# Converting 20 of 36 weight blocks to halved numbers by a shift and a sign function

## Chip, cores and metric

One core of one Trainium2 chip runs the whole program. The metric is the device time of one execution in microseconds (us), the median of several runs. Engines are named as in the profile: PE is TensorE (PEld its weight loads), DVE is VectorE, ACT is ScalarE, POOL is GpSimd, SP is the engine that issues most DMAs.

## What is computed

Attention over 4 batches, 8 heads, 576 positions and a head size of 64, in which each row keeps only its 32 largest scores; then a dense gated layer `(x @ w_a) * (x @ w_b) @ w_out`; then a routed layer, in which each token goes to the one of 8 experts whose embedding is nearest.

```python
scores = q @ k.T / sqrt(D)                       # per batch and head
kth = partition(scores, -32)[..., -32]
attn = softmax(where(scores >= kth, scores, -1e9))
x = (attn @ v) as 2304 x 512
x = ((x @ w_a) * (x @ w_b)) @ w_out              # d_ff = 1536
e = argmax(normed(x) @ normed(expert_emb).T / tau)
out = gate * (relu(x @ w1[e]) @ w2[e])
```

`w_a`, `w_b`, `w_out` arrive as 64-bit floating-point numbers; all else is of 32 bits.

## The kernel before

The work runs in three stages. In the first, 144 rows of attention (a row is 128 queries against 576 keys) pass through all engines in a pipeline. For each row TensorE makes the scores (L373), ScalarE copies them out of PSUM (`s<-tr`, L374), VectorE finds the 32 largest by four MAX8 and three MATCH_REPLACE8 (L394, L397) and sets a threshold `bi` (L399), ScalarE and POOL apply it and the softmax (L406, L409, L411), TensorE turns the weights (L428) and ScalarE copies them (`wt<-tr`, L431). Each fourth or fifth row closes with the product with `v` (L469), which ScalarE copies too (L472, L457). The dense layer (`moe1`, 9 groups of 256 tokens, 12 column blocks `f` in each) is woven into the rows' gaps on TensorE, and the routing of its tokens follows. The last stage is the experts, after the attention is over.

The order of instructions on PE, DVE, ACT and POOL in the first stage is written out by the program itself (`manual_schedule`): the main loop goes through 144 steps and in each step calls pieces of each row's work in fixed slots. SP's queue is ordered by priorities. An engine works through its queue strictly in order.

The weights of the dense layer are converted once, beside the first 36 or so rows, in 36 blocks of 128x512 numbers (`Blocks`): `order` is a0, b0, a1, b1, then six blocks of `w_out` (o0 to o5), then a2, b2, o6, a3, b3, o7 and so on, at last a11, b11. Below, a, b and o stand for `w_a`, `w_b` and `w_out`. Each block takes these steps:

- SP loads the block (`fetch`, L523) into one of two buffers `raw64`. The load of a block waits until all readers of the block two before it are done.
- ScalarE takes the upper three bits of each number's low word (`w64r<-raw`, L543, the low half of a 32-bit word).
- VectorE shifts the high word left by 3 and clears the two upper bits (`w64t<-raw`, L546), and takes sign and upper exponent bit from the high word into the upper half of `w64r` (L547).
- POOL adds both as whole numbers (`x1T<-w64t,w64r`, L551): that is the number in 32 bits.
- ScalarE rounds it (`wab` or `wo<-x1T`, L559), TensorE forms the rest (L562, L563), ScalarE copies that (L564), and SP stores blocks of a and b to DRAM (`wab_d`, L566).

The steps of a block are called from the main loop: `conv.open()` runs the first one (L543) in slot 3 of a step, just ahead of a copy of scores; `conv.start()` runs VectorE's at the step's end; `conv.stage()` runs the rest in slots 0, 2 and 4. Until step 16 a block is taken up every second step, then two a step.

The gated product is made at L743 (L741 for the first two blocks of the first group): a copy of both products `a` and `b` out of PSUM into `gab`. The layer's output is copied out of PSUM in `route` (L773).

Of the kernel before, what the change touches and what calls it, by code (L numbers as in the profile page):

```python
# [10 lines left out]
F32 = mybir.dt.float32  # L11
F32R = mybir.dt.float32r
BF16 = mybir.dt.bfloat16
I32 = mybir.dt.int32
I16 = mybir.dt.int16
U32 = mybir.dt.uint32
AF = mybir.ActivationFunctionType
OP = mybir.AluOpType
# [50 lines left out]
OB = 3  # L69
NTF = 1  # L70
RGL = 0.8
ET = 0
FX = (0, 5)
EK = 1
# [13 lines left out]
def fused_kernel(  # L88
# [18 lines left out]
    pe, dve, act, pool, sp = nc.tensor, nc.vector, nc.scalar, nc.gpsimd, nc.sync  # L107
# [4 lines left out]
    NT, DM = out.shape  # L112
# [94 lines left out]
    with ExitStack() as ph:  # L207
# [292 lines left out]
        class Blocks:  # L500
# [34 lines left out]
            def block(self, k):  # L535
                i, f = self.order[k]
                raw = self.raw[k]
                if raw.dtype == F32:
                    x = raw
                else:  # L540
                    lo, hi = raw[:, :, :, 0], raw[:, :, :, 1]
                    r = wk.tile([P, KC, P, 2], I16, name="w64r", bufs=TB)
                    act.activation(r[:, :, :, 0], lo.bitcast(U32), AF.Copy, scale=2.0**-29)  # L543
                    yield
                    t = wk.tile([P, KC, P], I32, name="w64t", bufs=TB)
                    dve.tensor_scalar(t, hi, 3, 0x3FFFFFFF, op0=OP.logical_shift_left, op1=OP.bitwise_and)  # L546
                    dve.tensor_scalar(r[:, :, :, 1], raw.bitcast(I16)[:, :, :, 3], -0x4000, None, op0=OP.bitwise_and)  # L547
                    self.fetch(k + 1 + RB)
                    yield
                    x = mk.tile([P, KC, P], F32, name="x1T", bufs=XB)  # L550
                    pool.tensor_tensor(x.bitcast(I32), t, r.rearrange("p a n t -> p a (n t)").bitcast(I32), op=OP.add)  # L551
                    yield
                if i < 2:
                    wt = mk.tile([P, 2, KC, P], F32R, name="wab", bufs=WB)
                    self.tiles[i, f] = wt
                    hi, lo = wt[:, 0], wt[:, 1]
                else:
                    hi, lo = (wo[:, a, f].rearrange("p (c j) -> p c j", c=KC) for a in range(2))
                act.activation(hi, x, AF.Copy)  # L559
                yield  # L560
                p = ps.tile([P, 512], F32, name="tr", bufs=NTR)
                pe.matmul(p, ident, x.rearrange("p c j -> p (c j)"), start=True, stop=False)  # L562
                pe.matmul(p, minusr, hi.rearrange("p c j -> p (c j)"), start=False, stop=True)  # L563
                act.activation(lo, p.rearrange("p (c j) -> p c j", c=KC), AF.Copy)  # L564
                if i < 2:
                    sp.dma_start(wab_d[i, f], wt.bitcast(F32).rearrange("p a c j -> p (a c j)"))  # L566

            def need(self, *block):
                while not self.ready(*block):
                    self.start()  # L570
                    self.stage()

            def ready(self, *block):
                return block in self.order[: sum(a == 4 for a in self.at)]
# [25 lines left out]
                        self.at[k] += 1  # L600

        conv = Blocks()

        routes = []
        routed = []
# [42 lines left out]
        def moe1(G):  # L648
# [12 lines left out]
            def tick():  # L661
                if pend:
                    pend.pop(0)[1]()  # L663

            def second(f, tiles=(0, 1)):
                while pend and pend[0][0] <= f:
                    tick()
                hi, lo = gs[f]
                if gi == 0:
                    conv.need(2, f)  # L670
                for t in tiles:
                    ts = slice(t * P, (t + 1) * P)
                    if f == 0:
                        px[t] = mp.tile([P, DM], F32, name="x1", bufs=2)
                    for i, (g, w) in enumerate(((lo, 0), (hi, 1), (hi, 0))):
                        pe.matmul(  # L676
                            px[t], g[:, ts], wo[:, w, f], start=(f == 0 and i == 0), stop=(f == NF - 1 and i == 2)
                        )
                    if f == NF - 1:
                        r = route(g0 // P + t, px[t])  # L680
                        next(r)
                        routes.append(r)
                        debt[1] = 0.0
                    tick()
                    yield 0.64
# [22 lines left out]
            for f in range(NF):  # L708
                nxt = todo[1][1] if len(todo) > 1 and todo[1][0] <= now[0] else None
                if f >= (NF - 4 if gi else NF - 1) and nxt:  # L710
                    nxt.inputs()
                if f + LA < NF:
                    G.load()
                elif nxt:
                    nxt.load()
                if gi == 0:
                    conv.begun = f
                    while now[0] < NRW and not (conv.ready(0, f) and conv.ready(1, f)):
                        yield None
                    for i in range(2):  # L720
                        conv.need(i, f)
                    ws[f] = [conv.tiles[i, f] for i in range(2)]
                ab = mk.tile([P, 2, GN], F32, name="gab")
                p = None if f in begun else mp.tile([P, 2, 256], F32, name="ab", bufs=2)
                ps_ = begun[f] if f in begun else [p[:, 0], p[:, 1]]
                for i, wt in enumerate(ws[f]):
                    terms = [(a, x, c) for (a, x) in TERMS1 for c in range(KC) if f not in begun or c == KC - 1]
                    for j, (a, x, c) in enumerate(terms):
                        pe.matmul(  # L729
                            ps_[i],  # L730
                            wt[:, a, c, :],
                            xg[x][:, c, :],
                            start=(j == 0 and f not in begun),
                            stop=(j == len(terms) - 1),
                        )
                        if j % 4 == 3 and (i == 0 or j < 11):
                            tick()
                            yield 4 * N / 2400
                if f in begun:
                    for i in range(2):  # L740
                        act.activation(ab[:, i], ps_[i], AF.Copy)  # L741
                else:
                    act.activation(ab, p, AF.Copy)  # L743
                recent[0] = ab
                yield 4 * N / 2400
                hi = mk.tile([P, GN], F32R, name="gh", bufs=LAG + 2)
                lo = mk.tile([P, GN], F32R, name="gl", bufs=LAG + 2)
                gs[f] = hi, lo
                pend.append((f, lambda: None))
                pend.append((f, partial(pool.tensor_tensor, ab[:, 0], ab[:, 0], ab[:, 1], op=OP.mult)))  # L750
                pend.append((f, lambda: None))
                pend.append((f, partial(act.activation, hi, ab[:, 0], AF.Copy)))
                pend.append((f, lambda: None))
                pend.append((f, partial(pool.tensor_tensor, lo, ab[:, 0], hi.bitcast(F32), op=OP.subtract)))
                if f >= LAG:
                    yield from second(f - LAG)
# [4 lines left out]
            for tiles in ((0,), (1,)) if gi == len(GROUPS) - 1 else ((0, 1),):  # L761
                for f in range(NF - LAG, NF):
                    for _ in range(6 if nxt else 0):
                        yield next(nxt[2])
                    for _ in range(NTF if tiles[0] >= ET else 0):
                        tail[0]()
                    yield from second(f, tiles)

        def route(ch, p):
            tk = mk.tile([P, 2], I32, name="tk", bufs=4)  # L770
            token_ids(tk, ch)
            xr = mk.tile([P, RW], F32, name="xr")
            act.activation(xr[:, :DM], p, AF.Copy)  # L773
            x1T = mk.tile([P, KC, P], F32, name="x1T", bufs=XB)
            st = mk.tile([P, 8], F32, name="st")
            act.activation(x1T.rearrange("p c j -> p (c j)"), xr[:, :DM], AF.Square, accum_out=st[:, 0:1])
# [75 lines left out]
        def background(budget, final=False):  # L852

            debt[0] = min(debt[0] + budget, DEBT) if not final else final
            while debt[0] > 0 and (todo or (final and routes)):
# [15 lines left out]
                spent[0] += used  # L871
                if routes and debt[1] > (RGL if todo and todo[0][1].gi == len(GROUPS) - 1 else RGAP):
                    debt[1] = 0.0
# [66 lines left out]
        for step in range(-AHEAD_L, NRW + TL + 5):  # L940
# [64 lines left out]
            i = step - (TL0 if step < S1 else TL)  # L1005
            if i != turned[0] + 1:
                i = -1
# [37 lines left out]
            if 0 <= i < NRW:  # L1045
                next(tg, None)
                b, pr, part, first, last, kind, c, slot = rows[i]
                t = live.pop(i)
# [26 lines left out]
    with ExitStack() as ph:  # L1075
# [52 lines left out]
        def bank(name):  # L1128
            turns[name] += 1
            return banks[turns[name] % len(banks)].tile([P, 512], F32, name=name, bufs=2 if name == "h" else 1)  # L1130
# [189 lines left out]
        for e in range(1, NE):  # L1320
            r = NE - e
# [13 lines left out]
            if e + 1 < NE:  # L1335
                yT = wx.tile([P, KC, cap], F32, name="yT", bufs=1)[:, :, :n]
                for d in range(KC):
                    p = bank("y")[:, :n]
# [17 lines left out]
            else:  # L1356
                for t in range(NT3):
                    p = bank("y")
# [90 lines left out]
```

## Time and profile before

| | |
|---|---|
| median of 3 runs | 1251.49 us (1246.62 to 1252.79) |
| profiled execution | 1249.34 us, span of its instructions 1247.5 us |
| PE, PEld | busy 1134.9 (91%), 982.7 (79%) |
| DVE | busy 914.2 (73%), 2015 instructions |
| ACT | busy 822.5 (66%), 1970 instructions |
| POOL | busy 731.1 (59%) |
| mean granted clock of TensorE | 0.966 of 2.4 GHz |

Shares of the whole span mix the three stages: DVE has almost nothing to do after 820 us. The windows view cuts the span into stretches and gives each engine's busy time in each. In the timeline a line has start, duration, engine, source line, operation and operands; `x2` is two instructions back to back, and a bracket at the end is the idle time ahead of the line and what ended it.

### The profile page before, as it was taken

Reading aid. Unit: us, or ns where it says so; the run is one execution under the profiler, and the core shown is the slowest. Engines: PE = TensorE matmul, PEld = TensorE weight load, DVE = VectorE, ACT = ScalarE, POOL = GpSimd, SP = SyncE. Lnnn points to the kernel's source line nnn. Section 1 sums busy time; section 2 is a strip of 40 time slices with the busy share of each in tenths; the row PEclk is TensorE's granted clock in tenths of the full one; section 3 lists DMA queues with packets and bytes.
Section 4 is the critical chain, followed back from the end, with each engine's and each line's share of the span. In section 5 each row is a group of like instructions: output and inputs, shape, how many; then the busy total and the mean of one; then the engine's idle time right before and its main releaser. Section 6 shows DMA issues by size and latency. Waiting matters only on the chain. (4 is left out here: it accounts for less than half of the span.)

```text
span 1247.5 us, 23919 instructions
## 1 busy us (share of the span) xinstructions
PE 1134.9 (91%) x8124; PEld 982.7 (79%) x8125; DVE 914.2 (73%) x2015; ACT 822.5 (66%) x1970; POOL 731.1 (59%) x1195
## 2 busy tenths in 40 slices
PE   5677798999999998999998999899999989999996
PEld 4445566787888887888787888777898868999995
DVE  8998999999999998998999898860110225655540
ACT  5777888888778887777877787663542434555441
POOL 5555698777777876776877677564554420232221
PEclk8788899999999999999999999899999989999998
DMA  7334567667775666667575667557987335565530
GB/s 235 118 123 144 193 198 257 224 215 223 252 228 148 191 222 218 181 203 220 159 204 169 205 191 220 186 155 226 325 296 210 110 124 207 177 218 207 184 102 27
DMA packets 129200, 240.05 MB, mean 192 GB/s; under 512 B 24896, under 2 KB 74176, under 8 KB 129074
## 3 DMA queue, kind: packets, MB, share of 16 engines
q1 hardware_dynamic: 125170, 228.74, 57.9%
q0 software_dynamic: 3904, 9.75, 2.1%
q8 instruction: 65, 1.06, 0.4%
q14 instruction: 61, 0.50, 0.1%
HBM read 198.38 MB, written 40.31 MB: 191 GB/s over the span
## 5 line engine op out<-in xcount | busy, mean ns | idle before, releaser
L394 DVE MAX8 t<-y 128x8 f32<-128x576 f32 x432 | 311.8, 749 | 2.7
L409 POOL TENSOR_TENSOR z<-s,z 128x576 f32<-128x576 f32 x144 | 206.2, 1432 | 73.0 <-ACT z L406 70.3
L397 DVE MATCH_REPLACE8 y<-t,y 128x576 f32<-128x576 f32 x288 | 213.9, 743 | 0.0
L729 PE MATMUL ab<-xg,wab 128*128 128x256 f32 x1398 | 208.8, 288 | 2.5 <-DMA wab<-wab_d 1.2
L729 PEld LDWEIGHTS ab<-xg,wab 128*128 128x128 f32 x1398 | 182.2, 189 | 5.4 <-DMA wab<-wab_d 1.4
L428 PE MATMUL tr<-ident,z 128*128 128x128 f32 x720 | 135.3, 288 | 49.0 <-ACT z L411 44.8
L729 PE MATMUL ab<-raw,wab 128*128 128x256 f32 x1152 | 173.8, 290 | 3.1 <-DMA wab<-wab_d 2.1
L374 ACT ACTIVATE s<-tr 128x288 f32<-128x288 f32 x288 | 117.8, 410 | 58.4 <-PE tr L373 35.1
L729 PEld LDWEIGHTS ab<-raw,wab 128*128 128x128 f32 x1152 | 151.7, 191 | 5.9 <-DMA wab<-wab_d 2.1
L431 ACT ACTIVATE wt<-tr 128x384 f32<-128x384 f32 (+2 forms) x320 | 127.9, 411 | 39.2 <-PE tr L428 38.1
L428 PEld LDWEIGHTS tr<-ident,z 128*128 128x128 f32 x720 | 89.6, 146 | 68.0 <-ACT z L411 56.8
L676 PE MATMUL x<-wo,gh 128*128 128x512 f32 x432 | 136.2, 397 | 0.0
L1155 POOL DMA_INDIRECT out_dram<-o,ids x24 | 33.1, 1378 | 169.7 <-ACT o L1154 118.0
L373 PE MATMUL tr<-kT,qT 128*128 128x288 f32 x512 | 123.8, 327 | 8.2 <-ACT s L374 5.1
L1102 DVE TENSOR_TENSOR u<-raw,u 128x1024 fp32r<-128x1024 f32 x64 | 76.1, 1221 | 69.2 <-ACT u L1101 47.2
L663 POOL TENSOR_TENSOR gl<-gab,gh 128x256 fp32r<-128x256 f32 x108 | 82.8, 767 | 55.0 <-ACT gh L663 45.8
L394 DVE MAX8 t<-s 128x8 f32<-128x576 f32 x144 | 107.0, 743 | 7.6 <-ACT s L374 7.6
L411 ACT ACTIVATE z<-z,bi 128x576 f32<-128x576 f32 x144 | 112.1, 778 | 0.3 <-POOL z L409 0.3
L406 ACT ACTIVATE z<-s,bi 128x576 f32<-128x576 f32 x144 | 111.3, 773 | 0.3 <-DVE bi L399 0.3
L663 POOL TENSOR_TENSOR gab<-gab 128x256 f32<-128x256 f32 x108 | 80.5, 745 | 51.0 <-ACT gab L743 42.8
L397 DVE MATCH_REPLACE8 y<-t,s 128x576 f32<-128x576 f32 x144 | 106.9, 742 | 0.0
L373 PEld LDWEIGHTS tr<-kT,qT 128*128 128x128 f32 x512 | 87.5, 202 | 18.2 <-ACT s L374 5.7
(201 smaller groups left out, 2244.3 us busy)
## 6 DMA issues: line engine op xcount, KB each, us to landing
wab<-wab_d SPq DMA_DIRECT2D x192, 512.0 KB, 4.6
raw<-in_moe_w_dram SPq DMA_DIRECT2D x28, 1024.0 KB, 5.4
wab_d<-wab SPq DMA_DIRECT2D x24, 512.0 KB, 4.7
kT<-kT_d SPq DMA_DIRECT2D x20, 576.0 KB, 5.7
vs<-in_v_dram SPq DMA_DIRECT2D x36, 256.0 KB, 3.1
kT_d<-kT SPq DMA_DIRECT2D x16, 576.0 KB, 4.6
raw<-in_moe_w_a_dram SPq DMA_DIRECT2D x12, 512.0 KB, 4.5
raw<-in_moe_w_b_dram SPq DMA_DIRECT2D x12, 512.0 KB, 4.7
```

What stands on the lines that cost most here:

```text
L373: pe.matmul(p, l, r, start=(i == 0), stop=(i == len(terms) - 1))
L374: act.activation(t.s[:, cs], p, AF.Copy, scale=SCALE)
L394: dve.max(v, cur)
L397: dve.match_replace(out=rest, in_to_replace=v, in_values=cur, imm_value=LOWEST)
L406: act.activation(t.w, t.s, AF.Relu, bias=t.bi[:, 1:2], scale=-HUGE)
L409: pool.tensor_tensor(t.w, t.s, t.w, op=OP.subtract)
L411: act.activation(t.w, t.w, AF.Exp, bias=t.bi[:, 0:1], accum_out=t.o.sm[:, t.slot : t.slot + 1])
L428: pe.transpose(pt[:, i * P : (i + 1) * P], t.w[:, k0 : k0 + P], ident)
L431: act.activation(th[:, sl, w], pv[:, :, src], AF.Copy)
L663: pend.pop(0)[1]()
L676: pe.matmul(px[t], g[:, ts], wo[:, w, f], start=(f == 0 and i == 0), stop=(f == NF - 1 and i == 2))
L729: pe.matmul(ps_[i], wt[:, a, c, :], xg[x][:, c, :], start=(j == 0 and f not in begun), stop=(j == len(terms) - 1),)
```

## The change

Twenty blocks are converted in another way: the twelve of `w_a`, and the first four (`f < F3`, F3 = 4) of `w_b` and of `w_out`. VectorE only shifts, without clearing the two upper bits, and no longer takes sign and exponent bit. In their place ScalarE applies the function Sign to the upper 16 bits of the number, read as bfloat16, and writes +1.0 or -1.0 in bfloat16 to the upper half of `w64r`. POOL's addition is the same; the sum is now half the number. The other 16 blocks stay as they were. Copies that exist already carry a factor 2 in their scale: the copy of `gab` where both products are halved or one is (`f < 4`), and the copy of the layer's output.

```diff
+F3 = 4
...
                     act.activation(r[:, :, :, 0], lo.bitcast(U32), AF.Copy, scale=2.0**-29)
+                    if i == 0 or f < F3:
+                        act.activation(r.bitcast(BF16)[:, :, :, 1], raw.bitcast(BF16)[:, :, :, 3], AF.Sign)
                     yield
                     t = wk.tile([P, KC, P], I32, name="w64t", bufs=TB)
-                    dve.tensor_scalar(t, hi, 3, 0x3FFFFFFF, op0=OP.logical_shift_left, op1=OP.bitwise_and)
-                    dve.tensor_scalar(r[:, :, :, 1], raw.bitcast(I16)[:, :, :, 3], -0x4000, None, op0=OP.bitwise_and)
+                    if i == 0 or f < F3:
+                        dve.tensor_scalar(t, hi, 3, None, op0=OP.logical_shift_left)
+                    else:
+                        dve.tensor_scalar(t, hi, 3, 0x3FFFFFFF, op0=OP.logical_shift_left, op1=OP.bitwise_and)
+                        dve.tensor_scalar(
+                            r[:, :, :, 1], raw.bitcast(I16)[:, :, :, 3], -0x4000, None, op0=OP.bitwise_and
+                        )
                     self.fetch(k + 1 + RB)
...
+        HALVED = 1.0 if w_a.dtype == F32 else 2.0
...
-                        act.activation(ab[:, i], ps_[i], AF.Copy)
+                        act.activation(ab[:, i], ps_[i], AF.Copy, scale=HALVED if f < F3 else 1.0)
...
-                    act.activation(ab, p, AF.Copy)
+                    act.activation(ab, p, AF.Copy, scale=HALVED if f < F3 else 1.0)
...
-            act.activation(xr[:, :DM], p, AF.Copy)
+            act.activation(xr[:, :DM], p, AF.Copy, scale=HALVED)
```

On VectorE, where blocks b2 (buffer 1168) and o6 (1182) are converted at the end of a step. Before:

```order
L397 MATCH_REPLACE y_1187<-t8_1188,y_1187 128x576
L546 TENSOR_SCALAR w64t_1257<-raw64_1168 128x512
L547 TENSOR_SCALAR w64r_1239<-raw64_1168 128x512
L546 TENSOR_SCALAR w64t_1260<-raw64_1182 128x512
L547 TENSOR_SCALAR w64r_1243<-raw64_1182 128x512
L394 MAX t8_1188<-y_1187 128x8
```

And now (lines have moved by 1 to 9; L550 is the shift alone, L552 and L553 the old pair):

```order
L398 MATCH_REPLACE y_1187<-t8_1188,y_1187 128x576
L550 TENSOR_SCALAR w64t_1258<-raw64_1168 128x512
L552 TENSOR_SCALAR w64t_1260<-raw64_1182 128x512
L553 TENSOR_SCALAR w64r_1244<-raw64_1182 128x512
L395 MAX t8_1188<-y_1187 128x8
```

b2 is among the 20, o6 is not: one instruction is gone, and the neighbours stand as before. This is so at all 20 places.

On ScalarE, slot 3 of the step in which the same two blocks are opened. Before:

```order
L431 ACTIVATE wt_1196<-tr_1227 128x2x128
L559 ACTIVATE wo_127<-x1T_1216 128x512
L543 ACTIVATE w64r_1239<-raw64_1168 128x512
L543 ACTIVATE w64r_1243<-raw64_1182 128x512
L374 ACTIVATE s_1220<-tr_1245 128x288
```

And now (L546 is the Sign):

```order
L432 ACTIVATE wt_1196<-tr_1227 128x2x128
L567 ACTIVATE wo_127<-x1T_1216 128x512
L544 ACTIVATE w64r_1239<-raw64_1168 128x512
L546 ACTIVATE w64r_1239<-raw64_1168 128x512
L544 ACTIVATE w64r_1244<-raw64_1182 128x512
L375 ACTIVATE s_1220<-tr_1246 128x288
```

The Sign of b2 stands between the reads of b2 and o6, ahead of the copy of scores. ScalarE has 20 instructions more and nothing else moved; PE and POOL have the same instructions in the same order. SP has as many DMAs, and some neighbours change places.

## Rows read from the trace of the kernel before

**Rows 1.** Windows view: stretch, its length, then busy time of each engine.

```profile
28.00:118.00 90.00, 59.99 (x339) 42.86 (x339) 85.58 (x197) 68.40 (x158) 51.50 (x68) 0.81 0.40 130
118.00:240.00 122.00, 106.50 (x668) 80.15 (x665) 117.21 (x241) 105.39 (x237) 95.66 (x111) 0.97 0.63 212
240.00:820.00 580.00, 552.18 (x4241) 476.69 (x4240) 543.73 (x1262) 450.94 (x1176) 418.27 (x741) 0.98 0.66 202
820.00:1247.00 427.00, 401.57 (x2822) 372.09 (x2820) 144.35 (x254) 182.65 (x370) 150.36 (x250) 0.99 0.56 185
```

**Rows 2.** Waits of ScalarE from 28 to 113: total, times, longest.

```profile
ACT wt L431 <- PE tr L428: 10.7, 15, 1.0
ACT xsb L472 <- PE tr L469: 3.3, 3, 2.2
...
ACT z L411 <- POOL z L409: 0.3, 1, 0.3
```

**Rows 3.** Tile view of w64t and w64r: durations in ns, least, median, most.

```profile
L546 DVE TENSOR_SCALAR w64t<-raw x36: 397/578/1645, 9.0 to 226.2; 128x512 int32<-128x512 int32 x36
L547 DVE TENSOR_SCALAR w64r<-raw x36: 444/464/1678, 9.4 to 227.0; 128x512 int16<-128x512 int16 x36
```

**Rows 4.** Groups of ScalarE's instructions, 0 to 240: busy, mean ns, idle before.

```profile
L374 ACT ACTIVATE s<-tr 128x288 f32<-128x288 f32 x76 | 31.0, 409 | 4.5 <-PE tr L373 4.0
L543 ACT ACTIVATE w64r<-raw 128x512 int16<-128x512 uint32 x36 | 27.5, 788 | 9.8 <-DMA raw<-in_moe_w_a_dram 3.7 <-DMA raw<-in_moe_w_out_dram 3.6 <-DMA raw<-in_moe_w_b_dram 1.6
...
L559 ACT ACTIVATE wab<-x1T 128x512 fp32r<-128x512 f32 x23 | 14.0, 639 | 2.8 <-POOL x1T L551 2.8
...
L457 ACT ACTIVATE xR<-tr 128x256 f32<-128x256 f32 x7 | 2.7, 384 | 1.2 <-PE tr L449 1.2
...
L179 ACT ACT_TABLE_LOAD x1 | 1.3, 1283 | 0.6 <-PEq L1429 0.6
```

**Rows 5.** Timeline of ScalarE, four waits before 75.

```profile
21.66 0.63 ACT L559 ACTIVATE wab<-x1T 128x512 fp32r<-128x512 f32 x1 [2.21 <-POOL x1T L551]
...
26.23 0.60 ACT L564 ACTIVATE wab<-tr 128x512 fp32r<-128x512 f32 x1 [1.29 <-PE tr L563]
...
50.43 0.38 ACT L472 ACTIVATE xsb<-tr 128x256 f32<-128x256 f32 x1 [2.21 <-PE tr L469]
...
72.23 0.38 ACT L472 ACTIVATE xsb<-tr 128x256 f32<-128x256 f32 x1 [0.56 <-PE tr L469]
```

**Rows 6.** Timelines of ScalarE, SP and VectorE at the hand-over near 112.

```profile
112.01 1.41 ACT L543 ACTIVATE w64r<-raw 128x512 int16<-128x512 uint32 x2
...
112.82 0.38 SPq L523 DMA_DIRECT2D raw<-in_moe_w_a_dram  x1
...
118.45 0.62 DVE L546 TENSOR_SCALAR w64t<-raw 128x512 int32<-128x512 int32 x1 [3.02 <-DMA raw<-in_moe_w_a_dram]
```

**Rows 7.** Timelines of VectorE, SP, ScalarE and TensorE at the hand-over near 140.

```profile
137.97 1.00 DVE L547 TENSOR_SCALAR w64r<-raw 128x512 int16<-128x512 int16 x1
138.87 0.40 DVE L546 TENSOR_SCALAR w64t<-raw 128x512 int32<-128x512 int32 x1
...
140.84 0.38 SPq L523 DMA_DIRECT2D raw<-in_moe_w_a_dram  x1
...
146.25 0.78 ACT L543 ACTIVATE w64r<-raw 128x512 int16<-128x512 uint32 x1 [2.01 <-DMA raw<-in_moe_w_a_dram]
...
147.33 0.85 PE L373 MATMUL tr<-kT,qT 128*128 128x288 f32 x2 [3.42 <-ACT s L374]
```

**Rows 8.** Waits of ScalarE for loads, 185 to 240.

```profile
ACT w64r L543 <- DMA raw<-in_moe_w_out_dram: 3.0, 1, 3.0
...
ACT w64r L543 <- DMA raw<-in_moe_w_b_dram: 1.6, 1, 1.6
ACT w64r L543 <- DMA raw<-in_moe_w_a_dram: 0.3, 1, 0.3
```

**Rows 9.** Timeline of TensorE near 227.

```profile
227.72 0.40 PE L373 MATMUL tr<-kT,qT 128*128 128x288 f32 x1 [2.02 <-ACT qT L350]
```

## The prediction

> **What bounds the kernel now.** I read the windows view first, then the waits of ScalarE, then the timeline at the places where one engine releases another. Times below without a unit are microseconds into the span.
>
> The stretches show three regimes [rows 1]. From 820 on VectorE is a third busy and TensorE is at 94%. From 240 to 820 both are full (TensorE 552.18 of 580, VectorE 543.73), so what arrives late at 240 stays late to the end. The conversion of the weights, which is what the change touches, lies before 240. From 28 to 118 VectorE is 95% busy (85.58 of 90) and ScalarE only 76% (68.40), which would make VectorE the bound.
>
> The waits of ScalarE say otherwise [rows 2]. Between 28 and 113 nearly all its idle time is for TensorE: 15 times it has just finished an exponential and waits until TensorE has turned it (10.7 in all), and some other products. Only 0.3 is for POOL, and nothing for VectorE or a DMA. Such a round trip begins and ends on ScalarE, so it does not shrink when VectorE gets faster: in this stretch ScalarE with its round trips runs as a chain of its own, just as fast as VectorE. One hand-over decides which of the two counts. At 112.01 ScalarE reads two blocks back to back. At 112.82, when the first read is over, SP issues the DMA of the next block. VectorE stands still for 3.02 until that block lands and starts at 118.45 [rows 6]. So at 118 VectorE is late because ScalarE was.
>
> After 118 the roles turn. VectorE's mask of a block that keeps it ends when SP issues the next load at 140.84, ScalarE waits 2.01 for that load, and TensorE then waits 3.42 for the scores that ScalarE copies behind it [rows 7]. Here a faster VectorE helps.
>
> **The change part by part.**
>
> *The mask that goes.* 20 of 36 VectorE instructions `w64r<-raw` disappear. Their median is 464 ns, and one that meets POOL at the memory takes 1.00 [rows 3, 7]. The one at 137.97 runs to 138.97, its successor starts at 138.87: 0.10 overlaps. So one is worth 0.36 alone and 0.90 in company. In the timeline 4 of the 20 take 1.00, as at 137.97: 16 x 0.36 + 4 x 0.90 = 9.4 of VectorE time, ten of the 20 before 110.
>
> *The shift that loses its second operation.* `w64t` keeps its operands, and its 397 ns at the least [rows 3] is the time of its 512 elements a partition; no row shows the same shift with one operation. Gain at most 0.1 each (2 in all), loss none that a row suggests; I take 0.
>
> *The sign that comes.* 20 ScalarE instructions are added, each behind its block's `L543` and ahead of a score copy. No row shows this function. It reads and writes 512 elements at the same spacing as `L543`, which takes 788 ns; in a pair the second adds 1.41 - 0.79 = 0.62 [rows 4, 6]. A plain copy of 512 takes 639 ns, 0.15 less [rows 4]. Bounds 0.47 and 0.79 (no overlap); I take 0.62, the row with the same layout. 20 x 0.62 = 12.4 of ScalarE time.
>
> *The scale in the copies.* Score copies `L374` already carry a scale: 409 ns for 288 columns, against 384 for 256 in `L457` without one [rows 4]. That is 25 ns for 32 more columns, so a scale costs nothing.
>
> *Queues.* TensorE and POOL keep every instruction in its place. SP issues as many transfers, with neighbours swapped while blocks are loaded; the loads of the later blocks keep their order. VectorE no longer writes half of `w64r`; POOL's addition then waits for the sign. POOL is a step behind ScalarE, which hides it, except for a block read directly ahead of its addition. I take 0, and up to 1 for the range.
>
> *The sum along the chain.* Three signs lie before 28. ScalarE's waits of 2.21 and 1.29 follow them [rows 5] and take them up. Seven come between 28 and the issue at 112.82. The one near 47 lies ahead of a wait of 2.21 for a product that does not depend on it, the one near 71 ahead of one of 0.56 [rows 5]: these two cost 0 and 0.06. The other five stand ahead of the exponential that starts a round trip, or (the last) ahead of SP's issue itself. 5 x 0.62 = 3.1, so the block that VectorE waits for lands 3.1 later. What VectorE has saved by then only lengthens its wait.
>
> From 118 to 140.84 VectorE is free of waits and loses three masks: 0.36 + 0.36 + 0.90 = 1.6. The load at 140.84 is issued 3.1 - 1.6 = 1.5 later. Behind it ScalarE runs the sign of that very block before it copies the scores: TensorE goes on at 147.33 + 1.5 + 0.6, so 2.1 later. Until about 190 one more mask of 0.90 counts on the way to a load, and the two signs there fall into ScalarE's wait of 3.0 [rows 8]: 1.2 late. The last four signs cost 2.5, of which ScalarE's waits of 0.3 and 1.6 for loads [rows 8] take up 1.9: 1.8 late. TensorE meets this where it waits for ScalarE at 227.72 [rows 9], and carries it to the end. 1249.34 of the profiled execution + 1.8 = **1251.1**. That execution lies 2.15 below the median of the three runs (1251.49), which spread over 6.2, so about 0.5% is what can be told from no change.
>
> With 0.47 for a sign the same path gives 3.1 - 0.75 = 2.35 at 118 and about 0.3 at the end (1249.6); with 0.79, 4.0 at 118 and about 3.5 at the end (1252.8).
>
> **The rivals.**
>
> *VectorE is the bound from the start to 240.* Then the signs find room on ScalarE and the masks' 9.4 come off: 1239.9, and 1238 if the shift gives its 2. For it: VectorE's 95% [rows 1], and 3.0 + 1.6 + 0.3 of ScalarE's time waiting for loads late in the conversion [rows 8]. Against it: rows 2 and 6. Chance 0.24.
>
> *The sign becomes the last reader of every halved block.* SP loads the next block only when the last reader of its buffer is done. At 112 that is ScalarE, at 140 VectorE [rows 6, 7]. If the 12.4 make ScalarE last in the second half too, its waits for loads move along instead of shrinking, and every sign counts, those before 28 included: 1249.3 + 12.4 = 1261.7. It decides from the point where ScalarE ends with a block more than one mask (0.36) after VectorE. For it: VectorE is done sooner with these blocks. Against it: ScalarE's waits there, 4.9 in rows 8 alone, show that it reads as soon as a block lands. Chance 0.15.
>
> *The sign needs another table.* The whole run before has one table load of 1283 ns [rows 4]. If the new function lay outside the loaded set, 20 signs between exponentials would want 40 loads: 40 x 1.283 = 51, so 1301. The changed program's list of ScalarE instructions has one load, as before. Chance 0.03. The Trainium skill's page "ScalarE: Activation LUTs", section "What ACT_TABLE_LOAD costs", puts a switch at about 2.66 us with the drain; by that figure the 40 would be an estimated 106 us, and no run here shows a switch.
>
> **How the numbers follow.** 0.58 for the forecast, 0.24, 0.15 and 0.03 for the rivals. The likeliest time is 1251.1. The range leaves out the tables and about half of the two other rivals' far ends: 1239 to 1260. Faster by over 0.5% (below 1245.2 from the median): the first rival and a little more, 0.25. Slower by over 0.5%: the second and third, 0.18. Within: 0.57.
>
> **What would show it.** Right: `w64r` on VectorE 16 times instead of 36; the sign near 0.8 alone and 0.62 in a row; before 118 VectorE idle by some 7 instead of 3, for ScalarE's scores or a load; ScalarE's waits for loads after 140 mostly gone; TensorE's busy time in 240 to 820 unchanged. Wrong: if VectorE's stretch up to 240 is 6 or more shorter, the round trips of rows 2 were slack after all; if SP's loads after 140 follow the sign, the second rival holds; more than one table load would be the third.

## The result and the profile after

The changed kernel takes 1258.0 us (median of 17 runs, 1252.4 to 1264.3) beside 1251.8 for the kernel before: ratio 1.0051, 95% interval [1.0036, 1.0066], so 6.2 slower between the medians. The forecast was 1251.1 and no change; the range to 1260 held the time, the sign was wrong. Two later measurements of the same kernel gave 1.0047 and 1.0049. Times without a unit are microseconds.

The windows of the profiled execution, as in [rows 1] (span 1257.1, before 1247.5):

```profile
28.00:118.00 90.00, 58.55 (x317) 41.38 (x315) 81.94 (x185) 69.30 (x159) 48.55 (x64) 0.79 0.37 121
118.00:240.00 122.00, 105.28 (x642) 78.54 (x641) 112.00 (x225) 109.88 (x244) 92.60 (x109) 0.96 0.65 213
240.00:820.00 580.00, 550.98 (x4217) 476.08 (x4216) 540.36 (x1257) 451.55 (x1175) 419.49 (x739) 0.98 0.66 202
820.00:1257.00 437.00, 411.51 (x2895) 379.62 (x2893) 153.46 (x273) 189.02 (x385) 153.99 (x260) 0.98 0.56 184
```

VectorE is less busy in both early stretches (81.94 against 85.58, 112.00 against 117.21) and the kernel is slower: the freed time has become waiting. The tile view gives the parts, as in [rows 3]:

```profile
L546 ACT ACTIVATE w64r<-raw x20: 744/770/827, 11.3 to 232.5; 128x512 bf16<-128x512 bf16 x20
L553 DVE TENSOR_SCALAR w64r<-raw x16: 449/475/1691, 94.2 to 232.7; 128x512 int16<-128x512 int16 x16
...
L550 DVE TENSOR_SCALAR w64t<-raw x20: 402/428/1511, 8.5 to 230.7; 128x512 int32<-128x512 int32 x20
```

The sign takes 0.77 and delays ScalarE's next instruction by 0.62 (timelines below), as forecast. The second operation of the shift cost nothing: the least time is 402 ns with one and 397 with two. The copies that got a scale take 598 ns at the median before and after. There is still one table load.

What changed most is who releases the load of the block after next. SP's queue from 0 to 250, first before, then after (total, times, longest):

```profile
SPq L523 <- DVE w64r L547: 65.7, 24, 8.3
...
SPq L523 <- ACT s L374: 10.9, 10, 3.6
...
SPq L523 <- ACT w64r L543: 3.4, 4, 1.7
```

```profile
SPq L524 <- ACT s L375: 30.6, 17, 4.5
SPq L524 <- DVE w64t L550: 23.1, 10, 5.9
SPq L524 <- DVE w64r L553: 16.9, 7, 6.1
...
SPq L524 <- ACT w64r L544: 7.8, 5, 3.4
SPq L524 <- ACT w64r L546: 5.1, 3, 2.3
```

Before, VectorE's mask ended most of these waits (65.7 beside 14.3 for ScalarE). Now ScalarE ends 25 of them (43.5) and VectorE 17 (40.0); where the score copy behind the sign is named, it only starts as the sign ends. By their ends in the timeline, ScalarE is the last reader of 13 of the 34 blocks whose buffer is used again before the change, and of 28 after it.

ScalarE's own waits for loads between 118 and 245 fell from 8.9 to 2.2, as the prediction said they would; first before, then after:

```profile
ACT w64r L543 <- DMA raw<-in_moe_w_a_dram: 3.7, 4, 2.0
ACT w64r L543 <- DMA raw<-in_moe_w_out_dram: 3.6, 2, 3.0
...
ACT w64r L543 <- DMA raw<-in_moe_w_b_dram: 1.6, 1, 1.6
```

```profile
ACT w64r L544 <- DMA raw<-in_moe_w_a_dram: 2.2, 2, 1.5
```

**How late ScalarE is.** The start of its first exponential of a row (L411, now L412) lets one follow a run through the whole conversion. The table gives, for four rows, how much later it starts than in the profiled execution of before, and the ratio of the times with its interval. At row 38 the conversion is over. One profiled execution wanders by 2 or 3 in this stretch: read patterns here, totals from the ratio.

| run | row 0 (26.7) | row 14 (105.3) | row 18 (136.7) | row 38 (271.6) | ratio of times |
|---|---|---|---|---|---|
| the change | +2.5 | +5.3 | +8.0 | +7.2 | 1.0051 [1.0036, 1.0066] |
| e5, the same | +1.6 | +3.4 | +5.8 | +6.4 | 1.0047 [1.0023, 1.0071] |
| e17, the same | +2.9 | +6.3 | +9.0 | +8.6 | 1.0049 [1.0024, 1.0073] |
| e1, SP's order restored | -0.6 | +0.8 | +3.2 | +3.6 | 1.0019 [1.0002, 1.0035] |
| e11, the same | +0.4 | +4.7 | +7.4 | +6.7 | 1.0039 [1.0022, 1.0056] |
| e2, SP's order alone | +0.7 | +2.0 | +3.3 | +3.7 | 0.9991 [0.9976, 1.0006] |
| e3, signs and all masks | +1.2 | +2.7 | +5.8 | +9.0 | 1.0044 [1.0029, 1.0058] |
| e4, no masks, no signs | -0.3 | -2.5 | -2.7 | -6.9 | (other routing) |
| e6, signs of b and o | +1.2 | +3.4 | +5.8 | +4.8 | 1.0026 [1.0004, 1.0048] |
| e7, signs of a | +0.4 | +1.1 | +1.1 | +3.2 | 1.0008 [0.9990, 1.0027] |
| e8, late pairs | +0.5 | +0.6 | +0.6 | +1.8 | 1.0018 [0.9995, 1.0041] |
| e9, signs in the wait | +1.5 | +4.1 | +6.9 | +6.7 | 1.0036 [1.0016, 1.0056] |
| e10, as e7, SP's order swapped | +1.7 | +0.2 | +1.7 | +2.5 | 1.0025 [1.0007, 1.0043] |
| e12, as e1 without b2, o2 | +1.1 | +5.1 | +7.1 | +7.4 | 1.0044 [1.0023, 1.0064] |
| e13, one sign (b2) | +0.8 | +1.8 | +2.6 | +2.5 | 1.0018 [1.0000, 1.0036] |
| e14, one sign (a0), order swapped | +2.0 | +3.4 | +3.4 | +2.7 | 1.0017 [0.9999, 1.0036] |
| e15, early signs twice | +2.3 | +12.3 | +15.5 | +15.7 | 1.0112 [1.0083, 1.0142] |
| e16, late signs twice | +2.5 | +6.8 | +9.5 | +16.3 | 1.0101 [1.0069, 1.0134] |

### The profile page after: what moved, and what is told of

The parts are those of the page before. It is cut to its first block, busy times and chain, and to the rows that moved or that the text cites. A ratio compares the mean times of both kernels' runs of the same rounds, so it can differ in the third digit from the quotient of the medians.

```text
span 1257.1 us, 23920 instructions
## 1 busy us (share of the span) xinstructions
PE 1141.3 (91%) x8124; PEld 986.9 (79%) x8125; DVE 910.6 (72%) x1995; ACT 835.5 (66%) x1990; POOL 729.4 (58%) x1195
## 5 line engine op out<-in xcount | busy, mean ns | idle before, releaser
L412 ACT ACTIVATE z<-z,bi 128x576 f32<-128x576 f32 x144 | 112.0, 778 | 0.0
L374 PEld LDWEIGHTS tr<-kT,qT 128*128 128x128 f32 x512 | 88.5, 204 | 17.9 <-ACT s L375 5.9
```

The lines of the kernel that those rows point to most:

```text
L374: pe.matmul(p, l, r, start=(i == 0), stop=(i == len(terms) - 1))
L412: act.activation(t.w, t.w, AF.Exp, bias=t.bi[:, 0:1], accum_out=t.o.sm[:, t.slot : t.slot + 1])
```

## The experiments

**The start: SP's order (e1, e2).** In the changed kernel SP issues the load of a1 ahead of the last piece of k. e1 puts it back:

```diff
-with tc.high_priority(offset=2 * FG if len(self.raw) < EL else FG):
+with tc.high_priority(offset=2 * FG if len(self.raw) < EL else FG // 2 if len(self.raw) == 2 else FG):
```

> The changed kernel with the third load of a weight block (a1) put back behind the last pieces of k in SP's queue, as before the change; every other engine keeps the changed kernel's instructions. Theory: the 6.4 us have three parts, 2.4 from that swap at the start, 2.8 from signs between 28 and 112 us, and about 1.2 from signs that have become the last reader of a buffer after 118. Then this run is 2.4 under the changed kernel: 1255.6, ratio to before 1.003, and ScalarE's first x1T copy is back near 21.7 us. Rival A, the signs alone cost and a later start is taken up by waits: 1258.0, ratio 1.005. Rival B, the queue's order is the whole loss: 1251.8, ratio 1.000.

e2 makes the swap in the kernel before, with `FG + FG // 2` in the same place:

> The kernel before with only that swap: SP puts the load of block a1 ahead of the last pieces of k; no sign, all masks. Theory of three parts: 1251.8 + 2.4 = 1254.2, ratio 1.002, and ScalarE is 2.4 late from about 24 us to the end. Rival A, the start is taken up by waits: 1251.8. Rival B, the order is the whole loss: 1258.

e1 lost less than the change (1252.2 beside 1250.5); e2 lost nothing that the times can tell. The timelines of SP, POOL and ScalarE show what the order does. The change:

```profile
12.63 1.03 SPq L256 DMA_DIRECT2D kr<-in_k_dram  x1
13.77 0.53 SPq L524 DMA_DIRECT2D raw<-in_moe_w_a_dram  x1
14.34 0.52 SPq L256 DMA_DIRECT2D kr<-in_k_dram  x1
...
19.12 0.67 POOL L228 TENSOR_SCALAR ks<-kr 128x576 fp32r<-128x576 f32 x1 [5.37 <-DMA kr<-in_k_dram]
...
24.09 0.63 ACT L567 ACTIVATE wab<-x1T 128x512 fp32r<-128x512 f32 x1 [4.22 <-POOL x1T L559]
```

e1 and e2:

```profile
12.56 1.23 SPq L256 DMA_DIRECT2D kr<-in_k_dram  x2
13.89 0.52 SPq L524 DMA_DIRECT2D raw<-in_moe_w_a_dram  x1
...
16.70 0.67 POOL L228 TENSOR_SCALAR ks<-kr 128x576 fp32r<-128x576 f32 x1 [3.03 <-DMA kr<-in_k_dram]
...
21.69 0.63 ACT L567 ACTIVATE wab<-x1T 128x512 fp32r<-128x512 f32 x1 [1.89 <-POOL x1T L559]
```

```profile
12.60 0.50 SPq L523 DMA_DIRECT2D raw<-in_moe_w_a_dram  x1
13.15 1.29 SPq L255 DMA_DIRECT2D kr<-in_k_dram  x2
...
17.99 0.67 POOL L227 TENSOR_SCALAR ks<-kr 128x576 fp32r<-128x576 f32 x1 [4.34 <-PE tr L373]
```

The load of a1 is 512 KB, the last piece of k 16 KB. Where the load is ahead of that piece in SP's queue, the piece lands later: the last packets of k move until 15.7 in e1, and until 17.9 in e5, which is the change measured again. POOL's scaling of k waits for the piece, its addition x1T comes behind that, and ScalarE waits 4.22 for x1T instead of 1.89.

The load of a1 needs the buffer of a0, whose last reader is now the sign, and the texts below take it (as theory F) that SP stands waiting for that sign. The timelines do not show this. The sign of a0 ends at 12.1 and the load is issued at 13.77, only 0.1 after SP is done with the piece of k ahead of it, as in e1. What the sign changes is the order that the program writes for SP: in e2 the load is ahead of both small pieces of k and is issued at 12.60; with the sign added it comes between them and is issued at 13.2 to 13.8, and the last piece comes behind it.

**Again, and with half of the signs (e5, e10, e11).**

> The changed kernel as it is, once more, beside the next three runs on the same chip, since the run with SP's order restored lost 2.4 where the changed kernel had lost 6.4, and the swap alone on the kernel before cost nothing (-1.4 between the medians, interval -3.0 to +0.8). Theory F, the swap costs only together with the sign: the load of a1 waits for the sign of a0 (ends at 12.1 us in place of 11.4) and the last piece of k waits behind that load: ratio near 1.005 again (1.004 to 1.006), row 0 again about 2.5 late. Rival G, chips or single starts differ and the start has no part in it: ratio near 1.002, row 0 less than 1 late.

> As e7 (only the twelve a blocks with shift and sign), but with SP's order as the changed kernel has it: the load of a1 ahead of the last piece of k. Theory F, with the sign of a0 ahead of that load the swap costs 2 to 3: ratio 1.003 beside e7's 1.0008, POOL's second ks not before 18.5, row 0 at 28.4 to 29.2. Rival L, the swap costs only the 1.3 that e2's trace shows and the medians can't tell it: ratio 1.001, ks near 18.0.

> e1 once more, beside e9 and e10 on one chip. The theory as it stands: ratio 1.002 (1.000 to 1.0035), ks at 16.6 to 17.8, row 0 at 26 to 28. If it comes out at 1.004 or more, SP's order has no part in the loss and e1 was low by chance.

**The smallest form of it (e14):** the kernel before, SP's order swapped, and one sign, that of a0, ahead of its L543, into a place that L543 then overwrites.

> The kernel before with SP's swapped order (as e2) and a single sign added, that of a0 at 10.6 us, ahead of its L543; all masks kept. Theory F: the load of a1 waits for it, the last piece of k is issued behind that load, POOL's second ks starts at 18.4 to 19.1 (16.6 to 17.8 with the order of before, 18.0 with the swap alone), and row 0 is 1.6 to 2.5 late: ratio 1.001 to 1.002. Rival L: ks at 18.0 as with the swap alone, row 0 at 27.5, ratio 0.999 to 1.000.

```profile
13.31 0.54 SPq L523 DMA_DIRECT2D raw<-in_moe_w_a_dram  x1
13.90 0.56 SPq L255 DMA_DIRECT2D kr<-in_k_dram  x1
...
18.61 0.67 POOL L227 TENSOR_SCALAR ks<-kr 128x576 fp32r<-128x576 f32 x1 [4.95 <-DMA kr<-in_k_dram]
```

In the seven executions with swap and sign POOL starts that scaling between 18.6 and 19.5, in ten with that load behind k between 16.6 and 17.8, in e2 at 17.99. So theory F has the times right, though not the reason. In e9, whose load of a1 comes later still, it starts at 18.16; why is not shown. The price of the order: row 0 is late by 1.6 to 2.9 in the seven (mean 2.2), in the ten by -0.6 to 1.2 (mean 0.5), so 1.7. The three ratios of the change average 1.0049 and those of e1 and e11 1.0029, which is 2.5, with an interval of 2 on each run; the times alone don't prove it.

**What the masks and the signs are worth apart (e3, e4).** e3 adds the 20 signs to the kernel before and keeps all masks; e4 drops the 20 masks and adds no sign.

```diff
+if i == 0 or f < 4:
+    act.activation(r.bitcast(BF16)[:, :, :, 0], raw.bitcast(BF16)[:, :, :, 3], AF.Sign)
 act.activation(r[:, :, :, 0], lo.bitcast(U32), AF.Copy, scale=2.0**-29)
```

> The kernel before with the 20 signs added on ScalarE, each ahead of its block's L543 and written to a place that L543 then overwrites; VectorE keeps all 36 masks and POOL's additions read the same values. Theory of three parts: 2.8 before 112 as in the changed kernel, then VectorE's masks end last with a buffer as before, so that the signs after 140 fall into ScalarE's waits for loads (4.9 are there) and cost little: 1251.8 + 2.8 + about 0.7 = 1255.3, ratio 1.003. Rival C, every sign counts wherever it stands: 17 signs at 0.62 to 0.77 = 10.5 to 13, 1262 to 1265. Rival D, VectorE is the bound and the signs find room: 1251.8.

> The kernel before without VectorE's mask in the 20 blocks and without a sign in its place: ScalarE's L543 writes the whole word, so that these weights lose their sign and the output is another. It leaves out the sign alone; loads, shifts, additions and products are all there, and the swap in SP's early order is kept out. The part up to 820 us is to be compared, since other tokens may go to other experts after that. Theory of three parts: nothing gained before 112, where ScalarE's round trips set the pace; after 118 three masks of 1.6 in all and perhaps one or two more of 0.4 to 0.9: 1.6 to 3 earlier at 240, about 1249.5. Rival D, VectorE is the bound from 28 on: 9 earlier, 1242.4. Rival E, nothing hangs on VectorE's masks: 1251.8.

e3 came out above the theory's size (+5.6 between medians, expected 3.5). Part of that is its own doing: its sign writes the place that L543 then overwrites, and such a sign holds L543 back by 0.82 and not 0.62, which makes 20 of them 4 dearer. Its trace loses 3.2 more between rows 18 and 38, where the signs were to vanish in waits. e4's whole time can't be read, since it routes other tokens to other experts (2059.6 in all), but until 820 the work is the same. It gains little up to row 18, beyond a stretch near 50 (below), and 4.2 between rows 18 and 38. e4 also makes ScalarE's read of these blocks shorter, since it writes whole words (0.68 instead of 0.79, some 0.6 of the 4.2). All of it comes behind row 20 (-2.7 at rows 18 and 20). So the masks were on the path late, for some 3.6 where the forecast counted 0.9, and not before, where it counted 1.6 between 118 and 140; this is read from one execution.

**Which signs cost (e6, e7, e8).** SP's order restored, signs of b and o only (e6, up to 138), or of a only (e7, most after 105); e8 converts only a7 to a10 and b7 to b10 by sign.

> SP's order restored, and only the eight blocks b0 to b3 and o0 to o3 converted by shift and sign (the a blocks keep the mask; the copy of gab doubles both products, the output's copy does not): signs up to 90 us, then b2 at 118 and b3 at 138 us. With e1 at +2.4 of which its trace shows some 1.4 by row 14 (105 us, counted from row 0) and 2.4 between rows 14 and 18. Theory H, a sign costs wherever ScalarE's chain sets the pace, which is before 118: +2.5 to +3, 1253, ratio 1.002. Rival I, the loss lies with the signs of the a blocks, after 105: 1250.5, ratio 1.000.

> SP's order restored, and only the twelve a blocks converted by shift and sign (F3 = 0): a0 and a1 before 28 us, none until a2 at 105, then one about every 12 us. Theory H: the second half is about even, each sign of 0.6 against a mask of 0.4 to 0.9: 1250.5, ratio 1.000. Rival I: ScalarE becomes the last reader of each of these buffers (17 of 22 blocks after 105 in the changed kernel against 5 before), so each sign counts nearly in full against masks that had counted only where VectorE was last: +2 to +3, 1253, ratio 1.002.

> The kernel before with shift and sign only in the eight blocks a7 to a10 and b7 to b10 (180 to 220 us), where in the kernel before VectorE ends with a block 1.4 to 3.1 after ScalarE and ScalarE then waits for loads (3.0, 1.6 and 0.3). A sign pays only where VectorE ends with the block more than a sign (0.62) later than ScalarE: here it should, eight masks of 0.36 to 0.9 go and the signs fall into the waits: 3 to 5 earlier, 1247, ratio 0.997. Rival J, the waits for loads have another cause (the load itself, the two buffers) and nothing moves: 1250.5. Rival I, each sign counts: slower by 2, 1252.5.

e6 and e7 went as theory H had it: +3.3 and +0.5 between the medians. e8 was a miss. In its trace each sign delays ScalarE by 0.62, the waits for loads take some back (8.9 become 4.5), and the sum stays positive: +1.2 between rows 18 and 38. A likely reason, which no run isolates, is that ScalarE's waits there were partly its own doing, since the loads follow its reads. An engine that waits for a load does not thereby have room for as much work ahead of the next load.

**Signs inside the round trip (e9).** Until step 16 the sign runs behind the exponential, while TensorE turns the weights, and the next load is issued behind it.

```diff
-    if i == 0 or f < F3:
-        act.activation(r.bitcast(BF16)[:, :, :, 1], raw.bitcast(BF16)[:, :, :, 3], AF.Sign)
+    sign = partial(act.activation, r.bitcast(BF16)[:, :, :, 1], raw.bitcast(BF16)[:, :, :, 3], AF.Sign)
...
+            with tc.high_priority(offset=FG):
+                conv.sign()
             for slot_, g in enumerate((tg, sg, tg, mg, sg)):
```

> SP's order restored, and until step 16 each sign moved from its place ahead of the scores to the next step, behind the exponential whose weights TensorE then turns, so that it runs inside ScalarE's wait for that round trip; the load of the block after next is issued behind it. Later blocks as in the changed kernel. Theory H: the ten or so signs before 112 cost ScalarE's chain most of the 2.4 of e1; moved into waits of 0.64 they cost next to nothing, and masks that go bring a little: 1.000 or below, 1250 to 1253 beside a kernel before of 1250 to 1253, and ScalarE not later at row 14 than at row 0. Rival K, what counts early is that the buffer is freed later and so the load comes later: the sign is later still, so ratio 1.003 or more, with VectorE or ScalarE waiting for raw.

No gain over e11, measured beside it, though the sign now fits into the wait. TensorE's timeline of e9 shows one new price:

```profile
53.24 0.51 PE L374 MATMUL tr<-kT,qT 128*128 128x288 f32 x2
54.63 2.06 PE L576 MATMUL tr<-x1T,ident 128*128 128x512 f32 x2 [0.88 <-POOL x1T L565]
55.71 1.42 PE L577 MATMUL tr<-wo,minusr 128*128 128x512 f32 x1
```

POOL's addition needs the sign, so x1T comes later, TensorE waits 0.88 for it where it had not waited, and the same pair of products takes 2.06 instead of 1.10 in the kernel before: the granted clock was 0.50 from 55 to 58, the lower level of 1.2 GHz.

**TensorE's clock (e12, e13).** That pattern is in the change too. In the windows of single microseconds behind the turn of row 15, e6 (with the sign of b2) and e7 (without):

```profile
118.00:119.00 1.00, 0.42 (x4) 0.42 (x5) 1.00 (x4) 0.53 (x2) 0.30 (x2) 1.00 0.91 279
119.00:120.00 1.00, 1.00 (x8) 1.00 (x7) 0.54 (x2) 0.49 (x1) 1.00 (x1) 0.65 1.08 380
120.00:121.00 1.00, 1.00 (x7) 1.00 (x6) 0.76 (x2) 0.89 (x2) 0.94 (x3) 0.50 0.84 291
121.00:122.00 1.00, 1.00 (x6) 1.00 (x6) 1.00 (x3) 1.00 (x3) 0.73 (x1) 0.50 0.25 66
```

```profile
117.00:118.00 1.00, 1.00 (x11) 1.00 (x10) 0.87 (x3) 0.81 (x3) 1.00 (x3) 1.00 1.07 366
118.00:119.00 1.00, 1.00 (x11) 0.79 (x11) 0.71 (x2) 1.00 (x3) 0.77 (x3) 1.00 0.59 207
```

The third figure from the right is TensorE's granted clock: it falls to 0.50 in e6, behind a wait of 2.91, and stays at 1.00 in e7, behind 2.29. ScalarE's copy of xsb then comes 6.7 behind that turn instead of 5.2. It fell so in all ten executions that had the sign of b2 among others, and of the eight without it in e2 alone.

> e1 (SP's order restored) without the signs of b2 and o2: these two blocks keep the mask, and the copy of gab doubles for f = 0, 1 and 3 only. Theory M: the sign of b2 lengthens TensorE's wait for z at row 15 to 2.2 to 3.1, behind which the granted clock fell to 0.5 in all seven runs that had this sign; the product with v then ended 1.5 later. So here the stretch from that turn to the copy of xsb is 5.2 again, not 6.7, with a granted clock of 1.00, and the time is 0.6 + 1.5 = 2 under e1 and e11 (which were at 1.0019 and 1.0039): about 1.001. Rival N, the clock falls there by chance or from elsewhere (it fell in the run with the order alone too): still near 6.7 and 1.003.

> The kernel before with a single sign added, that of b2 at 112 us, ahead of its L543 and overwritten by it; all masks kept. Theory M: the turn of row 15 waits 0.62 more, the clock falls behind it, and row 16 is 0.6 + 1.5 = 2.1 later than row 14 beside the kernel before (relative lateness); 1.0015 in the time if nothing takes it up. Rival N: 0.6 later, the clock as before, time within 0.05%.

Neither bears theory M out. e13 waited 2.59 and kept its clock. e12 kept it there too (5.2, 1.00), but it fell to 0.50 from 138 to 140 instead, and the time did not improve. So the clock falls behind waits of TensorE at several places in this stretch, in every execution, and this fall costs 1.5; a given fall can't be put down to a given sign. The kernel before has its own: the clock is at 0.50 from 47 to 49, ScalarE's wait of 2.21 at 50.43 in [rows 5] follows it, and all but three of the runs are 1.2 to 2.4 less late at row 4 than at row 2. The Trainium skill's page "TensorE: Matmul & The Clock Gate", section "What's actually happening", says that at the start of one kernel the number of matmuls at the lower clock is run-variable. Two executions here show the like in the midst of one: in e1 and e11, one kernel, the mean clock from 28 to 118 is 0.84 and 0.75, and row 14 is late by 0.8 and 4.7.

**The price of a sign, many times over (e15, e16).** To get out of that scatter, signs are written twice: seven between 28 and 118, or the nine of a3 to a11.

```diff
-if i == 0 or f < F3:
+for _ in range(2 if k in (3, 4, 5, 6, 7, 10, 11) else 1 if i == 0 or f < F3 else 0):
```

> The changed kernel with seven signs written twice to the same place: b1, o0 to o3, a2 and b2, all that lie between 28 and 118 us. Theory H: in the trace each sign moved ScalarE's chain by 0.62; seven more cost 7 x 0.62 = 4.3, less what two waits take up (0.6 to 1.2), beside the changed kernel of the same call: 3.1 to 4.3 slower, ratio to before about 1.008. Rival O, the signs cost nothing by themselves and the loss is the clock's and the start's: within 1 of the changed kernel. Rival P, each longer wait also brings a fall of the granted clock (1.5 at 119 us): 7 or more slower.

> The changed kernel with the nine signs of a3 to a11 written twice. The prediction's view of this stretch: ScalarE's waits for loads (4.9 from 185 to 240 in the kernel before) take up a sign or most of it: 0 to 2.5 slower than the changed kernel. Second rival of the prediction, the sign has become the last reader of these buffers and each counts: 9 x 0.62 = 5.6 slower, ratio to before about 1.009, and ScalarE's waits for loads do not shrink further.

> The changed kernel once more, beside e15 and e16: ratio to before 1.004 to 1.006; in the trace of one execution a sign moves ScalarE's chain by 0.62 wherever it stands before 118 us, whatever the clock does in it.

Against e17 the medians moved by +7.7 (1267.4) and +6.4 (1266.1). A second sign into the same place starts only when the first is done, so it adds more than 0.62; ScalarE's timelines of one block, e17 and e16:

```profile
220.20 0.78 ACT L544 ACTIVATE w64r<-raw 128x512 int16<-128x512 uint32 x1 [1.18 <-DMA raw<-in_moe_w_a_dram]
220.85 0.75 ACT L546 ACTIVATE w64r<-raw 128x512 bf16<-128x512 bf16 x1
221.46 0.39 ACT L375 ACTIVATE s<-tr 128x288 f32<-128x288 f32 x1
```

```profile
225.69 1.44 ACT L544 ACTIVATE w64r<-raw 128x512 int16<-128x512 uint32 x2
226.97 1.59 ACT L546 ACTIVATE w64r<-raw 128x512 bf16<-128x512 bf16 x2
228.44 0.38 ACT L375 ACTIVATE s<-tr 128x288 f32<-128x288 f32 x1
```

From the start of the first sign to the next copy it takes 1.47 instead of 0.61, on average 0.82 more. Nine of these are 7.4, and row 38 is 7.7 later than in e17: every second sign counts, and the waits for loads take up next to nothing more (at this block one of 1.18 goes, and the lateness is back by row 38; in all they are 2.0 in e17 and 2.7 in e16). Seven are 5.7, and from row 0 to row 18 e15 loses 7.1 more than e17: each counts, and 1.4 comes on top, by the wait of TensorE and the clock behind it or by chance. e16 shows what one more sign costs in the changed kernel, in which ScalarE is already the last reader and the waits are already short. It does not say that the first signs met no room: at row 20 a wait took part of them (below).

## Why the prediction was wrong

- *ScalarE's chain as the bound from 28 to 112, and 0.62 for a sign on it*: right as a mechanism. e4 gains nothing there that is not the clock's, and e15's doubled signs all count. The change loses 2.8, 1.8 and 3.4 between rows 0 and 14 in its three executions (mean 2.7), where 2.5 was forecast (four of the five signs lie ahead of row 14). That the size fits so well is partly luck: between rows 2 and 4 they win 1.6 on the kernel before, whose clock falls there, and elsewhere they lose 4.2. The wait of 2.21 near 50, in which a sign was to vanish, came from that fall.
- *"Queues … I take 0, and up to 1"*: failed. The swap of neighbours on SP costs 1.7 at row 0, because the 512 KB of a1 now move ahead of the last 16 KB of k, for which POOL and then ScalarE wait. The prediction counted the transfers and did not ask what waits for the one that was put behind. Its two waits of 2.21 and 1.29 that were to take up the first signs did so (row 0 at -0.6 and +0.4 in e1 and e11), but not this.
- *The sum after 118*: failed, and it is the larger part. 2.5 late at row 14 was to become 1.8 at the end. Measured from row 14 to row 38: 1.9, 3.0 and 2.3 later (mean 2.4) where 0.7 less was forecast, so 3.1 off. Row by row, in the mean of the three, the 3.1 has three parts:
  - Row 16 loses 1.5 by the clock's fall near 119, which no term held.
  - "From 118 to 140.84 VectorE is free of waits and loses three masks" put VectorE's masks on the path there and gave the signs of b3 and a4 no price. The runs show ScalarE's chain instead: rows 18 and 19 lose 0.6 each, and row 20 wins 1.4 back, because ScalarE's wait of 2.01 for a load [rows 7] shrinks to between 0.5 and 0.8. The masks are not it, since e4 without them wins nothing there and e3 with all of them wins 1.2. Up to row 20 that is 0.2 won where 1.0 was forecast (1.6 less a sign).
  - From row 20 on 0.6 is lost where 0.3 was to be won. Two terms missed there, and they nearly cancel, which is luck. The phrases "the two signs there fall into ScalarE's wait of 3.0" and "take up 1.9" had the signs nearly free, while with the masks gone the waits are short (from 170 on 3.0 in e4, 6.3 before), and a further sign counts in full (e16). And one mask of 0.90 was counted, while e4 puts the masks at some 3.6.
- Together: 2.3 at row 0, 2.7 and 2.4 make the 7.4 that the three executions are late at row 38 on average. Between the medians it is 6.2. The two can't be compared more closely: the three end 9.6, 9.1 and 11.1 late, and after row 38 nearly every run, whatever its edit, falls further behind the profiled execution of before (by 2.5 at the median), which lies 2.5 under the median of its kernel.
- *The second rival, "the sign becomes the last reader of every halved block"*: half right. ScalarE is the last reader (28 of 34 blocks), and a further sign counts (e16). But its waits for loads did shrink (8.9 to 2.2), and its price of 1261.7 is too high, because it let the masks bring nothing and every sign ahead of row 0 count.
- *The first rival, VectorE as the bound*: false before 118, true in part after it (e4). *The table switch*: false.

What stays open is how much of the 6.2 is the clock's; its falls move from run to run, and no run here could hold it fixed. The parts above are read from single executions, each good to 2 or 3; what the times themselves show is that signs added in either half cost (e15, e16).

## What to carry over

Two engines that read the same buffer can both be on the path of its next load: taking work from the one that ends last only helps until the other ends last, and idle time "waiting for a load" is not all room for work that stands ahead of the next load. Where a change swaps two transfers on one queue, ask how large the one in front is and who waits for the one behind: 16 KB behind 512 KB came some 2 later here. Look at both times before saying that one waited for the other: the load of a1 needed the sign's buffer, yet the buffer was free before its turn came. And a term of 0.6 per instruction on a chain is worth doubling in an experiment, since one run here can't tell less than 2 us.

## What the runs showed of the hardware

An ACTIVATE that follows another on ScalarE starts 0.15 before the profiled end of the first when they write to different places (0.77 long, 0.62 apart), and 0.03 after it when both write to the same place (e15, e16; 0.82 from start to start in e3). TensorE waited 2.59 at one place and kept its clock (e13), and 2.27 at the same place and lost it (e17).
